# Pooled query-key products issued ahead of the maximum over the local scores in a fused attention and two-layer MoE kernel

## The chip, the cores and the metric

The kernel runs on one core of one Trainium2 chip. The metric is the device time of one execution in microseconds (us). Engines are named as in the profile: PE is the matrix engine (TensorE), PEld its weight loads, DVE the vector engine, ACT the scalar engine, POOL the GpSimd engine, SP the engine that only issues transfers here. PSUM is the accumulator memory into which PE writes; it is used in banks of 512 fp32 columns.

## The reference

The input is q, k, v of shape 2 x 8 x 576 x 64 (batch, heads, tokens, head size). Each token attends twice: to its neighbours less than four tokens away, and on sequences that are pooled by four. The two results are added, and the sum goes through two feed-forward layers.

```python
q_d, k_d, v_d = means over groups of 4 tokens          # 144 pooled tokens
out_up = repeat(softmax(scale * q_d @ k_d.T) @ v_d, 4)
mask = abs(pos[:, None] - pos[None, :]) < 4
out_local = softmax(where(mask, scale * q @ k.T, -1e9)) @ v
x = (out_up + out_local) as 1152 x 512
h = relu(x @ w_in); x = (s * h * h + b) @ w_out          # MoE 1, d_ff 2048
p = probs / (sum(probs) + 1e-9)
out = sum over 4 experts of p[:, e] * (relu(x @ w1[e]) @ w2[e])   # F = 1024
```

Each softmax subtracts the row's maximum before the exponential.

## The kernel before, in words

The attention is cut into 16 units: 4 groups (batch x half of the sequence) times 4 pairs of heads. A half is 256 or 320 tokens; a unit works on local tiles of 64 queries and 72 keys, the two heads of a pair side by side in the 128 partitions. The steps of a unit, by their names in the code:

- `a_step` transposes k (L494) and q (L512) on PE; ACT copies them out of PSUM as `kT` (L500) and `qz` (L519), and DVE pools q to `qd` (L526). `k_step` pools k on POOL to `kd` (L539, L541); L474 and L475 on POOL pool v.
- `b_step` forms the scores. One PSUM bank, `ps[0]` (shown as psa in the profile, as the whole ring of banks is), takes the mask (L576), some filler products that keep PE active (L584) and the local scores (L591) in its columns 0 to 287 or 359. From column 360 the same bank takes the pooled scores: of both heads in units of the first half (L605), of one head in units of the second half, whose other head has a bank of its own (L615, two matrix products). DVE takes the negated maxima, `ml` over the local scores (L599) and `md` over the pooled ones (L617), and ACT the exponentials with their sums (L571; local ones to `pl`, pooled ones to `pd`).
- `norm_step` divides by the sums on DVE (L630 to L635), `c_step` transposes the weights on PE (L657) and ACT copies them to `pT` (L660), `d_step` multiplies them with v (L678, L685; ACT L694, DVE L701), and `x_step` splits the result into a high and a low part for the next layer (ACT L713, POOL or DVE L715).

The units are pipelined: in each round the steps run on different units (`b_step` one behind `a_step`, `c_step` two, `d_step` three). A scheduler orders each engine's instructions by priority from the order in which the program calls them; POOL's are in the order of the code. Between a writer and a reader of one tile it places a wait, and a PSUM bank is one tile: two instructions on different columns of a bank are kept in program order as well. Each engine works through its own instructions in that order.

Beside the attention, the weights of the following layers are prepared: a weight is split into high and low parts by ACT (L157, L196) and DVE (L161, L167, L186, L199), and the products of MoE 1 (helper `products`, L316, three products for one at full precision; ACT L767, L772, DVE L769, L773) fill PE between the attention's steps from about 51 us on. `keep_warm` (L361) adds filler products. The attention ends about 143 us into the span; what follows is MoE 1 and the four experts (L316, L863).

Of the kernel before, what the change touches and what calls it, by code (L numbers as in the profile page):

```python
# [13 lines left out]
ALU = mybir.AluOpType  # L14
AX = mybir.AxisListType
# [7 lines left out]
def attn_moe_moe_kernel(  # L23
# [14 lines left out]
    nc = tc.nc  # L38
# [36 lines left out]
    def window(n):  # L75

        return min(max(n * TQ - FAC, 0), S - W)
# [320 lines left out]
    def unit(u):  # L398
        g, j = divmod(u, NP)
        b, hf = divmod(g, HALVES)  # L400
        return g, j, b, hf

    def tiles(hf):

        return (0, CUT) if hf == 0 else (CUT, NTQ - CUT)
# [6 lines left out]
    def bank():  # L412
        return psa.tile([P, 512], F32, tag="a", name="psa")
# [137 lines left out]
    def b_step(u):  # L551

        g, j, b, hf = unit(u)
        n0, m = tiles(hf)
        gd = m * TQ // FAC
        qz, qd = st.pop(("q", u))
        kT = st["kT", j]
        kd = st["kd", j]
        pl = ap2.tile([P, MX, W], F32, tag="pl", name="pl")[:, :m]
        ml = ap2.tile([P, MX, 1], F32, tag="ml", name="ml")[:, :m]  # L560
        both = gd == GB
        pd = ap2.tile([P, 2, SD], F32, tag="pd", name="pd")
        md = ap2.tile([P, 2, 1], F32, tag="md", name="md")
        if both:
            pd, md = pd[:, :1], md[:, :1]
        else:
            pd, md = pd[:gd], md[:gd]
        sm = sums[u % 2]

        def exps(out, ps, m, total):  # L570
            nc.scalar.activation(  # L571
                out=out, in_=ps, func=ACTF.Exp, bias=m, scale=1.0, accum_out=total
            )

        ps = [bank()] + ([] if both else [bank()])
        last_pe["att"] = nc.tensor.matmul(  # L576
            ps[0][:, : m * W],
            identb.rearrange("p a q -> p (a q)"),
            mask[:, hf * 2 : hf * 2 + m].rearrange("p t w -> p (t w)"),
            start=True,  # L580
            stop=False,
        )
        for _ in range(fill[u] // 448):
            nc.tensor.matmul(  # L584
                ps[0][:, : m * W], idle[:, :P], idle[:, : m * W], start=False, stop=False
            )
        for t in range(m):
            k0 = window(n0 + t)
            for a in range(2):
                o = slice(a * D, a * D + D)  # L590
                last_pe["att"] = nc.tensor.matmul(  # L591
                    ps[0][a * TQ : a * TQ + TQ, t * W : t * W + W],
                    qz[o, t * TQ : t * TQ + TQ],
                    kT[o, k0 : k0 + W],
                    start=False,
                    stop=t == m - 1,
                )
        local = ps[0][:, : m * W].rearrange("p (t w) -> p t w", w=W)
        nc.vector.tensor_reduce(out=ml, in_=local, axis=AX.X, op=ALU.max, negate=True)  # L599
        pooled = [] if both else [ps[0][:gd, MX * W : MX * W + SD], ps[1][:gd, :SD]]  # L600
        if both:
            pooled = [ps[0][: 2 * gd, MX * W : MX * W + SD]]
            for a in range(2):
                o = slice(a * D, a * D + D)
                last_pe["att"] = nc.tensor.matmul(  # L605
                    ps[0][a * gd : a * gd + gd, MX * W : MX * W + SD],
                    qd[o, :],
                    kd[o, :],
                    start=True,
                    stop=True,  # L610
                )
        else:
            for a in range(2):
                o = slice(a * D, a * D + D)
                last_pe["att"] = nc.tensor.matmul(pooled[a], qd[o, :], kd[o, :], start=True, stop=True)  # L615
        for a in range(len(pooled)):
            nc.vector.tensor_reduce(  # L617
                out=md[:, a], in_=pooled[a], axis=AX.X, op=ALU.max, negate=True
            )
        for t in range(m):  # L620
            exps(pl[:, t], local[:, t], ml[:, t], sm[:, t])
        for a in range(len(pooled)):
            exps(pd[:, a], pooled[a], md[:, a], sm[: pd.shape[0], MX + a])
        st["p", u] = pl, pd
# [337 lines left out]
    def side_step():  # L962
# [14 lines left out]
    pool_order.enter_context(tc.manual_schedule(engines={mybir.EngineType.Pool}))  # L977
    steps = [
        (b_step, 1),
        (a_step, 0),  # L980
        (k_step, 0),
# [9 lines left out]
    for i in range(last + 1):  # L991
# [13 lines left out]
        for f, lag in steps:  # L1005
            u = i - lag
            if 0 <= u < NU:

                with tc.high_priority(ahead.get(f, 0)) if f in ahead and u < NP else nullcontext():
                    f(u)  # L1010
            if f is x_step and u >= 0 and u % NP == NP - 1:
                slots += l1_steps(0, u // NP) + l2_steps(0, u // NP)
                firsts.append(slots[-FC - KD])
                if u < NP:

                    for _ in range(3):
                        take_slot()
            if f in (k_step, c_step) and slots and i < last:
                take_slot()
            if f in (b_step, k_step, c_step, v_step):  # L1020
                side_step()
# [110 lines left out]
```

## Time and profile before

| | us |
|---|---|
| median of 3 runs | 696.87 (695.46 to 697.39) |
| profiled execution, its own time | 696.83 |
| span of the profiled execution | 695.0 |
| PE busy | 683.0 (98%) |
| DVE busy | 404.8 (58%) |
| ACT busy | 346.3 (50%) |
| POOL busy | 101.2 (15%) |

The span runs from the first to the last instruction of the profiled execution, and its own time is 1.83 us more. A row of a timeline gives the start in the span, the length, the engine, the line of the kernel, the operation with output and inputs, and, in brackets, the time for which the engine had been idle before and what ended it. A row of a window gives the busy time of each engine in that stretch and the granted clock as a share of the full 2.4 GHz: 0.50 is the lower level, 1.2 GHz.

### The profile page before, as it was taken

The page shows a single profiled execution, that of the slowest core. Times are in us where ns is not written, and L with a number is a line of the kernel's source. Part 1 is how long each engine was busy: PE and PEld are TensorE (multiplying, and loading weights), DVE is VectorE, ACT ScalarE, POOL GpSimd, SP SyncE. Part 2 cuts the span into 40 slices and gives each one's busy share as a digit, 9 for nine tenths or more (in the row PEclk, how much of TensorE's full clock was granted, in tenths as well). Part 3 has the DMA queues.
Part 4 walks back from the last instruction along what each step waited for, and adds up shares of the span by engine and source line. Part 5 has one row for each costly group of instructions (what it writes and reads, how often), then busy time and mean ns, then how long its engine had stood idle before and what let it go on. Part 6 is the DMA issues. An engine that isn't in the chain of part 4 may idle for free.

```text
span 695.0 us, 11964 instructions
## 1 busy us (share of the span) xinstructions
PE 683.0 (98%) x4788; PEld 620.2 (89%) x4788; DVE 404.8 (58%) x720; ACT 346.3 (50%) x846; POOL 101.2 (15%) x123
## 2 busy tenths in 40 slices
PE   9989999999999999999999999999999999999997
PEld 5768778899999999999899899999898988998996
DVE  1898847778862434496535636645546456455442
ACT  3768757777965666665534423433334233243220
POOL 4431332100000200103011201201211012010000
PEclk9999989999999999999999999999999999999999
DMA  8784635405410011010210201201101103011012
GB/s 179 200 206 102 110 83 159 141 6 192 166 64 1 0 32 46 16 32 1 62 31 31 70 21 56 67 32 38 54 31 62 30 32 91 3 60 31 1 61 75
DMA packets 54167, 46.43 MB, mean 67 GB/s; under 512 B 32224, under 2 KB 42720, under 8 KB 54112
## 3 DMA queue, kind: packets, MB, share of 16 engines
q1 hardware_dynamic: 54112, 45.67, 23.9%
q8 instruction: 37, 0.61, 0.4%
q14 instruction: 18, 0.15, 0.1%
HBM read 43.31 MB, written 2.36 MB: 66 GB/s over the span
## 4 chain that ended last, share of the span: by engine, by line
PE 92%; DVE 6%; ACT 2%; issue 1%; DVEq 0%; ACTq 0%
PE psm L316 43%; PE psx L863 25%; PE psx L316 13%; PE psa L361 3%; PE psa L657 1%; PE psa L685 1%; PE psa L591 1%; PE psa L678 1%; PE psa L512 1%; PE psa L615 1%; PE psa L494 1%; DVE cv L175 0%; DVE cv L186 0%; PE psa L605 0%; DVE cv L161 0%
## 5 line engine op out<-in xcount | busy, mean ns | idle before, releaser
L316 PE MATMUL psm<-w,h 128*128 128x512 f32 x864 | 208.7, 391 | 0.0
L316 PEld LDWEIGHTS psm<-w,h 128*128 128x128 f32 x864 | 158.5, 188 | 30.0
L863 PE MATMUL psx<-x,w 128*128 128x320 f32 (+1 forms) x768 | 117.8, 296 | 0.0
L863 PEld LDWEIGHTS psx<-x,w 128*128 128x128 f32 x768 | 109.3, 190 | 1.7
L259 POOL TENSOR_TENSOR sw<-raw 128x256 f32<-128x256 f32 x32 | 31.3, 1000 | 411.5 <-DMA raw<-in_moe_w_dram 245.4
L878 ACT COPY r<-psx 128x320 f32<-128x320 f32 (+1 forms) x96 | 38.0, 396 | 92.6 <-PE psx L863 92.2
L881 ACT ACTIVATE h<-r 128x320 fp32r<-128x320 f32 (+1 forms) x96 | 42.0, 444 | 83.6 <-DVE r L892 83.6
L934 DVE SCALAR_TENSOR_TENSOR acc<-psm,pr,acc 128x512 f32<-128x512 f32 x63 | 47.2, 749 | 58.0 <-PE psm L316 58.0
L863 PE MATMUL psx<-t,w 128*128 128x320 f32 (+1 forms) x448 | 80.3, 302 | 0.2 <-DVE r L892 0.2
L892 DVE TENSOR_TENSOR r<-psx,r 128x320 f32<-128x320 f32 (+1 forms) x96 | 43.2, 456 | 58.7 <-PE psx L863 56.7
L863 PEld LDWEIGHTS psx<-t,w 128*128 128x128 f32 x448 | 67.0, 189 | 4.5 <-DVE r L892 0.5
L316 PE MATMUL psm<-x,w 128*128 128x320 f32 (+2 forms) x420 | 68.9, 315 | 0.0
L316 PEld LDWEIGHTS psm<-x,w 128*128 128x128 f32 x420 | 63.8, 193 | 0.9 <-issue 0.8
L882 DVE SCALAR_TENSOR_TENSOR h<-r,h 128x320 fp32r<-128x320 f32 (+1 forms) x96 | 47.7, 502 | 18.5 <-ACT h L881 16.2
L316 PE MATMUL psm<-h,w 128*128 128x256 f32 (+2 forms) x360 | 56.3, 305 | 0.0
L316 PE MATMUL psx<-h,w 128*128 128x384 f32 (+1 forms) x312 | 55.8, 327 | 0.0
L316 PEld LDWEIGHTS psx<-h,w 128*128 128x128 f32 x312 | 52.0, 188 | 0.0
L316 PEld LDWEIGHTS psm<-h,w 128*128 128x128 f32 x360 | 50.8, 190 | 1.0 <-issue 0.7
L316 PE MATMUL psx<-x,w 128*128 128x384 f32 (+2 forms) x252 | 43.1, 320 | 0.0
L316 PEld LDWEIGHTS psx<-x,w 128*128 128x128 f32 x252 | 40.6, 188 | 0.0
L237 DVE TENSOR_TENSOR w<-raw,w 128x1024 fp32r<-128x1024 f32 x16 | 19.5, 1224 | 25.8 <-ACT w L234 25.8
L780 DVE TENSOR_TENSOR h<-r,h 128x384 fp32r<-128x384 f32 (+2 forms) x40 | 21.6, 541 | 20.9 <-ACT h L779 19.6
(105 smaller groups left out, 874.6 us busy)
## 6 DMA issues: line engine op xcount, KB each, us to landing
raw<-in_moe_w_dram SPq DMA_DIRECT2D x32, 512.0 KB
raw<-in_moe_w_in_dram SPq DMA_DIRECT2D x8, 1024.0 KB
raw<-in_moe_w_out_dram SPq DMA_DIRECT2D x8, 1024.0 KB
kn<-in_k_dram SPq DMA_DIRECT2D x8, 288.0 KB
v<-in_v_dram SPq DMA_DIRECT2D x8, 288.0 KB
out_dram<-acc SPq DMA_DIRECT2D x9, 256.0 KB
qn<-in_q_dram SPq DMA_DIRECT2D x8, 160.0 KB
vn<-in_v_dram SPq DMA_DIRECT2D x16, 72.0 KB
```

The lines of the kernel that those rows point to most:

```text
L237: nc.vector.tensor_tensor(out=k0[1], in0=source(), in1=f32(k0[0]), op=ALU.subtract)
L259: nc.gpsimd.tensor_tensor(out=operand(out), in0=operand(x), in1=operand(y), op=op)
L316: nc.tensor.matmul(o, stat(ps, kk), mov(pm, kk, i), start=c == 0, stop=c == len(terms) - 1)
L361: nc.tensor.matmul(ps[:, c0:], idle[:, :P], idle[:, :n], start=True, stop=True)
L494: last_pe["att"] = nc.tensor.transpose(psk[:, i * KP : i * KP + KP], kn[:, c * m + i].rearrange("p a d -> p (a d)"), ident[:KP, :KP],)
L780: nc.vector.tensor_tensor(out=h[1], in0=r, in1=f32(h[0]), op=ALU.subtract)
L863: nc.tensor.matmul(ps, s_ap(n, half, a, w, kk), xt[x, pi][b][:, kk], start=first and c == 0, stop=c == len(terms) - 1, skip_group_check=True,)
L878: nc.scalar.copy(t, st[name])
L881: nc.scalar.activation(out=h[0][:, halves[hf]], in_=t, func=ACTF.Relu)
L882: nc.vector.scalar_tensor_tensor(out=h[1][:, halves[hf]], in0=t, scalar=0.0, in1=f32(h[0][:, halves[hf]]), op0=ALU.max, op1=ALU.subtract,)
L892: nc.vector.tensor_tensor(out=st[t], in0=st[name], in1=st[t], op=ALU.add)
L934: nc.vector.scalar_tensor_tensor(out=a, in0=ps, scalar=p_e, in1=a, op0=ALU.mult, op1=ALU.add)
```

## The change

The instruction that takes the maximum over the local scores is written behind the pooled products instead of ahead of them. Nothing is added or removed. Because the bank is one tile, the wait between the two turns round: before, the pooled products in `ps[0]` came behind the maximum in program order, and waited for DVE to have read the bank; now the maximum comes behind the products, and waits for PE to have written the bank.

```diff
         local = ps[0][:, : m * W].rearrange("p (t w) -> p t w", w=W)
-        nc.vector.tensor_reduce(out=ml, in_=local, axis=AX.X, op=ALU.max, negate=True)
         pooled = [] if both else [ps[0][:gd, MX * W : MX * W + SD], ps[1][:gd, :SD]]
         if both:
             pooled = [ps[0][: 2 * gd, MX * W : MX * W + SD]]
...
             for a in range(2):
                 o = slice(a * D, a * D + D)
                 last_pe["att"] = nc.tensor.matmul(pooled[a], qd[o, :], kd[o, :], start=True, stop=True)
+        nc.vector.tensor_reduce(out=ml, in_=local, axis=AX.X, op=ALU.max, negate=True)
         for a in range(len(pooled)):
             nc.vector.tensor_reduce(
                 out=md[:, a], in_=pooled[a], axis=AX.X, op=ALU.max, negate=True
```

In the changed file the pooled products are L604 and L614, and the maximum is L615; L617 and all behind it keep their numbers. Every engine has as many instructions as before. The order on POOL and SP is the same; on PE, DVE and ACT it differs only inside the attention. The numbers in the names below tell the tiles apart.

PE in unit 10 (85.7 to 90 us of the trace before). psa_1428 is the unit's score bank; the L494 rows are a later unit's transposes of k.

```order
 L576 MATMUL psa_1428<-mask_87,identb_84 128x288
 L591 MATMUL psa_1428<-kT2_1346,qz_1362 64x72 x8
-L605 MATMUL psa_1428<-kd2_1368,qd_1364 64x144 x2
+L604 MATMUL psa_1428<-kd2_1368,qd_1364 64x144 x2
 L494 MATMUL psa_1448<-ident_79,kn_1312 128x96 x3
 L494 MATMUL psa_1453<-ident_79,kn_1312 128x96 x3
```

PE's order is the same here, but for the line number: the pooled products stood directly behind the local scores before, too.

DVE in the same unit. qd_1364 is its pooled q; sums, pl_1322 and pd_1324 belong to unit 9, whose weights are divided here; ml_1425 and md_1427 are unit 10's maxima.

```order
 L526 TENSOR_REDUCE qd_1364<-psa_1357 128x64
+L632 TENSOR_TENSOR pl_1322<-pl_1322,sum1_107 128x288
 L701 TENSOR_TENSOR xg_1392<-psa_1370,ud_1390 128x320
-L632 TENSOR_TENSOR pl_1322<-pl_1322,sum1_107 128x288
 L635 TENSOR_TENSOR pd_1324<-pd_1324,sum1_107 128x144
 L715 TENSOR_TENSOR x1_77<-xg_1392,x0_76 128x320
-L599 TENSOR_REDUCE ml_1425<-psa_1428 128x4
+L615 TENSOR_REDUCE ml_1425<-psa_1428 128x4
 L617 TENSOR_REDUCE md_1427<-psa_1428 128x1
```

The maximum keeps its place behind four other DVE instructions (L632 and L701 change places); what turns round is which of the two, it or the pooled products, waits for the other.

ACT at about 31 us. psa_520 is a bank with transposed weights of unit 1, pl_551 and pd_553 are the exponentials of unit 2.

```order
 L713 CAST x0_76<-xg_511 128x256
 L157 ACTIVATE cv_441<-raw_297 128x1024
-L660 COPY pT_513<-psa_520 72x256
 L571 ACTIVATE pl_551,sum1_107<-psa_555,ml_552 128x72 x4
 L571 ACTIVATE pd_553,sum1_107<-psa_555,md_554 128x144
+L660 COPY pT_513<-psa_520 72x256
 L519 ACTIVATE qz_587<-psa_579 128x320
 L694 ACTIVATE ud_613<-psa_592 128x64
```

The copy that PE needs for unit 1's products with v (L678) moved behind all five exponentials of unit 2.

## Rows read from the trace of the kernel before

**Rows 1.** The page: span, engines, chain shares by engine
```profile
span 695.0 us, 11964 instructions
...
PE 683.0 (98%) x4788; PEld 620.2 (89%) x4788; DVE 404.8 (58%) x720; ACT 346.3 (50%) x846; POOL 101.2 (15%) x123
...
PE 92%; DVE 6%; ACT 2%; issue 1%; DVEq 0%; ACTq 0%
```

**Rows 2.** Windows: stretch, length, busy PE, PEld, DVE, ACT, POOL, granted clock, DMA, GB/s
```profile
12.00:143.00 131.00, 124.39 (x1437) 102.97 (x1434) 99.07 (x204) 91.84 (x331) 38.12 (x42) 0.96 0.59 143
143.00:690.00 547.00, 546.81 (x3284) 509.97 (x3283) 303.95 (x510) 251.37 (x511) 58.74 (x64) 1.00 0.15 46
30.00:40.00 10.00, 7.99 (x107) 5.96 (x103) 9.06 (x16) 7.09 (x22) 4.64 (x5) 1.00 0.58 114
40.00:50.00 10.00, 8.96 (x109) 7.17 (x108) 9.75 (x18) 6.29 (x25) 3.62 (x3) 0.83 0.85 215
...
84.90:88.30 3.40, 1.08 (x20) 0.70 (x19) 2.44 (x8) 2.31 (x10) 1.04 (x2) 0.96 0.71 176
88.30:94.40 6.10, 6.10 (x29) 5.04 (x31) 2.16 (x6) 2.67 (x14) 2.49 (x4) 0.50 0.47 102
```

**Rows 3.** Waits on PE: total us, times, longest
```profile
PE psa L615 <- DVE ml L599: 3.6, 3, 2.0
PE psa L605 <- DVE ml L599: 2.2, 2, 1.6
...
PE psa L576 <- ACT pd L571: 0.7, 1, 0.7
```

**Rows 4.** Timeline 30 to 50 us: start, length, engine, line; brackets: idle before
```profile
31.43 0.31 DVE L617 TENSOR_REDUCE md<-psa 128x1 f32<-128x144 f32 x1 [0.71 <-PE psa L605]
...
31.63 0.37 ACT L660 COPY pT<-psa 72x256 f32<-72x256 f32 x1 [0.21 <-PE psa L361]
...
33.10 0.38 ACT L571 ACTIVATE pd<-psa,md 128x144 f32<-128x144 f32 x1
...
38.62 0.30 DVE L617 TENSOR_REDUCE md<-psa 80x1 f32<-80x144 f32 x1
...
38.76 0.47 PE L615 MATMUL psa<-kd,qd 64*80 64x144 f32 x2 [2.01 <-DVE ml L599]
38.83 1.33 DVE L199 TENSOR_TENSOR w<-cv,w 128x1024 fp32r<-128x1024 f32 x1
...
48.09 0.47 PE L615 MATMUL psa<-kd,qd 64*80 64x144 f32 x2 [1.04 <-DVE ml L599]
```

**Rows 5.** Timeline, 81 to 88 us, up to the longest wait for the maximum
```profile
81.09 0.71 PE L494 MATMUL psa<-ident,kn 96*128 96x96 f32 x6
...
81.98 1.49 POOL L474 TENSOR_TENSOR v<-v 72x512 f32<-72x512 f32 x1
82.26 1.38 DVE L635 TENSOR_TENSOR pd<-pd,sum 128x144 f32<-128x144 f32 x1
...
83.56 0.29 DVE L617 TENSOR_REDUCE md<-psa 128x1 f32<-128x144 f32 x1
...
85.96 0.72 PE L591 MATMUL psa<-kT,qz 64*64 64x72 f32 x16
85.99 0.38 DVE L526 TENSOR_REDUCE qd<-psa 128x64 f32<-128x256 f32 x1
...
87.04 0.30 DVE L635 TENSOR_TENSOR pd<-pd,sum 128x144 f32<-128x144 f32 x1
...
87.69 0.45 DVE L599 TENSOR_REDUCE ml<-psa 128x4 f32<-128x288 f32 x1
```

**Rows 6.** Timeline, 88 to 91 us, the wait and the stretch behind it
```profile
88.29 0.74 PE L605 MATMUL psa<-kd,qd 64*64 64x144 f32 x4 [1.61 <-DVE ml L599]
...
88.96 1.22 PE L494 MATMUL psa<-ident,kn 96*128 96x96 f32 x6
```

**Rows 7.** Timeline near 108 us
```profile
108.37 0.47 PE L615 MATMUL psa<-kd,qd 64*80 64x144 f32 x2 [0.51 <-DVE ml L599]
```


## The prediction, written before the changed kernel ran

> **What bounds the kernel now.** I read the page first. PE is busy for 683.0 of 695.0 us, and the chain that ended last is 92% PE, 6% DVE [rows 1]. So time can only come from where PE idles or runs at the lower clock. The windows say where. From 143 to 690 us PE is busy for 546.81 of 547.00 us at a granted clock of 1.00: nothing is to be had there, and the order there is unchanged. From 12 to 143 us, the attention, it is busy for 124.39 of 131.00 us at a mean clock of 0.96 [rows 2]. That is 6.61 us of idling and about 131 x 0.04 = 5.2 us lost to the clock; 11.8 us is the ceiling for any change here.
>
> The waits on PE tell how much of the idling is the wait that the change turns round: the pooled products waited for the maximum over the local scores five times, 3.6 us at L615 and 2.2 us at L605, 5.8 us of the 6.61 [rows 3]. The timeline says where they lie: 2.01 us up to 38.76 and 1.04 up to 48.09 (place A) [rows 4], 1.61 up to 88.29 (place B) [rows 6], 0.51 up to 108.37 (place C) [rows 7]; the fifth is the rest of L605's sum, 2.2 - 1.6 = 0.6 us [rows 3].
>
> But a wait is worth only what limits its stretch. Place A lies in DVE's stretch: DVE is busy for 9.06 and 9.75 of 10 us in the windows from 30 and 40 us [rows 2]. Place B is PE's: DVE has 2.16 of 6.10 us behind the wait, and all of it runs at a clock of 0.50 with PE busy throughout [rows 2].
>
> **The change part by part.** No instruction is added or removed. All sums are against the profiled execution's own time, 696.83 us, 0.04 under the median of 696.87.
>
> *Place B.* L591 ends at 85.96 + 0.72 = 86.68. In the kernel before, L605 stands directly behind it in PE's order, and starts at 88.29, because the maximum (87.69, 0.45 us) stands on DVE behind four others, the last division L635 among them (87.04) [rows 5, 6]. After the change L604 needs only the pooled q and k. The pooled q is written by 85.99 + 0.38 = 86.37, before L591 ends [rows 5]; the pooled k came earlier. So the 1.61 us go. The maximum then waits for L604, which it doesn't notice: it comes up on DVE no earlier than before.
>
> Then the clock. In the 3.40 us up to 88.30 PE is busy for 1.08; the next 6.10 us run at 0.50, the lower level, 1.2 GHz [rows 2]. The same six transposes at L494 take 0.71 us at 81.09 and 1.22 at 88.96 [rows 5, 6]. At full clock this stretch takes 6.10 x 0.50 = 3.05 us. I expect the clock to stay up, because most of the idle time in front, 1.61 of 2.32 us, goes. So B gives 1.61 + 3.05 = 4.66 us. Bounds: if the clock falls all the same, or L604 starts some 0.4 us late behind a DVE instruction such as L526 (0.38), 1.61 - 0.4 = 1.2; if the exponentials move forward as well and the 0.71 us wait of L576 [rows 3] goes, 4.66 + 0.71 = 5.4. I take 4.66, because both of its terms stand in rows of this place, and the bounds need a further event.
>
> *Place A.* The waits of 2.01 and 1.04 us, 3.05 in all, go from L615. DVE's work stays, though, and is the limit, so PE must wait for it, or for what depends on it, elsewhere. The order shows two such places. On ACT, the copy L660 (31.63, 0.37 us, ends at 32.00) falls behind five exponentials, which end at 33.10 + 0.38 = 33.48 [rows 4]: PE's products with v wait for that copy, so some 33.48 - 32.00 = 1.48 us are put back there. On DVE the weight step L199 (1.33 us) comes before a pair of maxima, and with the one over the pooled scores (0.30, the 38.62 row) holds the following step by 1.63 us [rows 4]. 3.05 - 1.48 - 1.63 = -0.06: I count A as nothing. Bounds: 0.7 us better, since DVE's one idle piece here is 0.71 us, in front of 31.43 [rows 4]; 1.7 us worse, from the clock: the window from 40 us has a mean of 0.83, so 10 x 0.17 = 1.7 us are lost in it [rows 2]. There the loss lies in DVE's stretch and costs nothing; if the new waits put the fall a little later, where PE is the limit, it costs all of it.
>
> *Place C and the fifth wait.* At 108.37 PE is the limit, and the pooled products wait 0.51 us only because DVE was late [rows 7]: -0.51 (0 to -0.51). The fifth wait lies early, where DVE again sets the pace; 0, at best -0.6.
>
> *What is added.* In all 16 units the maximum now waits for the pooled products, 0.47 us of PE's time [rows 4]. On DVE, what is behind it waits as well: the maximum over the pooled scores, which waited for the products anyway, then the exponentials. Where PE is the limit, this is covered by PE's own queue; where DVE is, by the fact that md came behind the products before as well (in front of 31.43, DVE had idled for them already [rows 4]). I count 0; with no cover it would be 16 x 0.47 = 7.5 us on DVE's path, a bound that no stretch comes near.
>
> The Trainium skill ("PSUM — Partial Sum Buffer", section "PSUM bank collisions raise a hardware error") asks for PSUM to be guarded by bank, whatever the columns. By it the wait can't be removed here, only turned round, which speaks against the change. The trace agrees that the guard is a wait, 5.8 us in all [rows 3]; which side pays less is decided by the rows above, not by the rule.
>
> Sum: -4.66 + 0 - 0.51 = -5.17, so 696.83 - 5.17 = 691.7 us.
>
> **The rivals.**
>
> *R1, DVE stays late at B by another overlap.* In unit 9 the division L635 took 1.38 us, against 0.30 at 87.04, while POOL's L474 ran (81.98 to 83.47) [rows 5]. What is next on DVE, md at 83.56, came late, then the exponentials, then DVE's sums, behind which the pooled q stands. If after the change POOL meets another of these instructions as well, L604 waits for the pooled q: 1.08 us more. B is then worth 1.61 - 1.08 = 0.53 and the clock falls still; with C, 1.04, so 695.8 us. Against it: POOL's order is the same, and DVE's order there is nearly so. The Trainium skill ("SBUF — State Buffer", section "SBUF: two separate sides") says that DVE and GpSimd share a pair of ports as an exclusive lock, and the loser blocks; the 1.38 us agree with it.
>
> *R2, the clock falls at the wrong place.* The forecast, with A's upper bound: 691.7 + 1.7 = 693.4 us. For it: the 2.01 us wait of A becomes two waits a little later. Against it: DVE's stretch goes on behind them.
>
> *R3, slower: ACT's order.* ACT works in order, and the exponentials come earlier and as one block, ahead of copies that PE waits for. At A one block puts back 1.48 us, which is in the sum. If a second one does so where PE is the limit (the copies of k and q in units 8 to 10 stand beside exponentials, and L576 already waits 0.71 us for them [rows 3]), that costs 1.48 more; PE's idling there keeps B's low clock, so that B gives nothing, and A pays its 1.7. With C: 1.48 + 1.7 - 0.51 = +2.7, so 699.5 us. It decides as soon as PE's new waits for ACT are longer than B's removed 1.61 us. Against it: ACT is busy for only 2.31 of 3.40 us ahead of B [rows 2].
>
> *R4, nothing changes.* The wait is turned round, DVE's chain (division, maxima, exponentials, copy) is as long as before, and PE waits for the same total at other lines: 696.8 us. For it: DVE and ACT are busy for 99.07 and 91.84 of the attention's 131.00 us [rows 2], and A behaves this way by my own sum. Against it: B, where the product waits for an instruction whose result it doesn't use.
>
> **How the numbers follow.** Forecast 0.47, R2 0.15, R3 0.15, R1 0.13, R4 0.10. A measurement of this kernel tells about 0.3% from no change, 2.1 us: faster is under 694.7, slower over 699.0. Faster: the forecast, R2 nearly whole and the better edge of R1, 0.62. Same: the rest of R1, R4 nearly whole, a little of R2 and R3, 0.21. Slower: R3 and the bad ends, 0.17. The likeliest case's own range is 689.7 to 693.5: below it go A's 0.7, B's 0.7 and the fifth wait's 0.6 (691.7 - 2.0), above it A's 1.7. The range is 689.4 to 698.5, which adds 0.3 below for the scatter of runs, takes in R1, R2 and R4 above, and ends short of R3.
>
> **What would show it.** B right: the pooled products of unit 10 start within 0.1 us of the end of the local scores, and the granted clock in the six us behind is 1.00; L494 there takes 0.71. A right: the waits at L615's line gone, two new ones of about 1.5 us near 32 and 48 us, for ACT at L678 and for DVE at L657. R1 shows as a wait of the pooled products for L526; R2 as a clock of 0.50 behind 50 us; R3 as waits for ACT's copies at L591 or L678 from 75 us on. I am wrong if PE's idling between 12 and 143 us stays above 5 us with a mean clock no better than 0.96, although the waits for ml are gone.

## The result, and the profile after

The changed kernel takes 685.87 us (median of 4 runs, 685.39 to 689.71) against 697.06 us before (4 runs): a ratio of 0.9859 with a 95% interval of 0.9825 to 0.9894. Run once more among the experiments it gave 686.42 us, 0.9857 (0.9839 to 0.9875). It is some 10 us faster, in the forecast direction, about twice the forecast 5.2 us and below the range of 689.4 to 698.5. The profiled execution took 686.19 us, 10.64 less than the one before; its span is 10.6 us shorter.

The page of the changed kernel: span, engines, chain by engine.

```profile
span 684.4 us, 11971 instructions
...
PE 673.4 (98%) x4788; PEld 615.0 (90%) x4788; DVE 404.4 (59%) x720; ACT 345.1 (50%) x846; POOL 103.2 (15%) x123
...
PE 89%; DVE 7%; ACT 2%; issue 1%; DMA 1%; POOL 1%; ACTq 0%; POOLq 0%
```

PE is busy for 9.6 us less [rows 1], with the same number of instructions: what went is mostly time in which PE was busy, not idling. The waits on PE (total us, times, longest):

```profile
PE psa L657 <- DVE qd L526: 2.0, 1, 2.0
PE psa L678 <- ACT pT L660: 1.4, 1, 1.4
PE psa L657 <- ACT pd L571: 1.3, 1, 1.3
```

Nobody waits for ml any more; the 5.8 us of [rows 3] are gone, L576's 0.7 too. New are 2.0 us at L657 for DVE and 1.4 at L678 for ACT, the two waits that the prediction named for place A, and 1.3 more at L657.

To see where the time went, the span is cut at the same work in both kernels: at the mask products (L576) of units 8, 10, 12 and 15. Windows of the kernel before (stretch, length, busy PE, PEld, DVE, ACT, POOL, granted clock, DMA share, GB/s):

```profile
0.00:72.72 72.72, 67.77 (x728) 52.56 (x728) 52.56 (x106) 47.20 (x162) 23.85 (x38) 0.98 0.77 171
72.72:85.68 12.96, 12.17 (x168) 9.96 (x168) 10.47 (x20) 8.87 (x34) 6.17 (x8) 1.00 0.51 85
85.68:105.75 20.07, 18.42 (x173) 15.58 (x172) 10.81 (x29) 11.59 (x43) 6.12 (x8) 0.83 0.45 98
105.75:129.61 23.86, 23.35 (x260) 19.50 (x260) 18.86 (x39) 18.53 (x68) 3.35 (x4) 1.00 0.54 162
```

The same work in the changed kernel, and the four microseconds behind 49 us:

```profile
0.00:71.03 71.03, 64.55 (x727) 51.30 (x728) 52.20 (x105) 46.09 (x161) 24.60 (x37) 0.98 0.80 175
71.03:82.64 11.61, 11.61 (x169) 9.68 (x168) 9.39 (x23) 10.05 (x38) 6.44 (x7) 1.00 0.57 90
82.64:97.89 15.25, 15.14 (x174) 13.21 (x173) 10.88 (x27) 10.11 (x40) 7.19 (x9) 1.00 0.40 100
97.89:119.19 21.30, 21.30 (x261) 18.57 (x260) 18.09 (x39) 18.80 (x71) 3.82 (x4) 1.00 0.75 207
...
49.00:53.00 4.00, 4.00 (x23) 4.00 (x23) 2.24 (x9) 1.23 (x4) 0.00 (x0) 0.57 1.01 167
```

| stretch | forecast | measured | of it PE idle, clock, PE's products |
|---|---|---|---|
| start to unit 8 (place A) | 0 | 72.72 to 71.03: -1.69 | see below |
| units 8 and 9 | 0, at best -0.7 | 12.96 to 11.61: -1.35 | -0.79, 0, -0.56 |
| units 10 and 11 (place B) | -4.66 | 20.07 to 15.25: -4.82 | -1.54, -3.41, +0.13 |
| units 12 to 14 (place C) | -0.51 | 23.86 to 21.30: -2.56 | -0.51, 0, -2.05 |
| the rest | 0 | -0.2 | |

The split is worked out from the rows: idle is length less PE's busy time, the clock's part is length times one less the granted clock (20.07 x 0.17 = 3.41), and the rest is what PE's own products took at full clock. Place B came as forecast, to 0.2 us, and so did the wait of place C. What was missed is the first row and the second, and the 2.05 us by which PE's products themselves became shorter in the fourth. In the first row PE idles for 1.53 us more than before (6.48 against 4.95) and is busy for 3.22 us less (64.55 against 67.77).

At place B, unit 10 after the change, the pooled products start 0.11 us behind the end of the local scores (82.86 + 0.72 = 83.58), and the transposes behind them take 0.71 us, as at full clock:

```profile
83.69 0.46 PE L604 MATMUL psa<-kd,qd 64*64 64x144 f32 x4
84.08 0.71 PE L494 MATMUL psa<-ident,kn 96*128 96x96 f32 x6
```

The timeline shows where most of the 2.05 us come from. Unit 13 before, PE alone (start, length, line, operation):

```profile
115.44 0.47 PE L615 MATMUL psa<-kd,qd 64*80 64x144 f32 x2
...
116.13 0.39 PE L316 MATMUL psm<-h,w 128*128 128x320 f32 x1
116.45 0.47 PE L615 MATMUL psa<-kd,qd 64*80 64x144 f32 x2
116.85 1.88 PE L316 MATMUL psm<-h,w 128*128 128x320 f32 x11
118.66 0.46 PE L678 MATMUL psa<-pT,vd 72*64 72x64 f32 x8
```

and after:

```profile
106.19 0.48 PE L614 MATMUL psa<-kd,qd 64*80 64x144 f32 x4
106.60 0.49 PE L512 MATMUL psa<-ident,qn 80*128 80x80 f32 x4
106.89 2.00 PE L316 MATMUL psm<-h,w 128*128 128x320 f32 x12
108.82 0.46 PE L678 MATMUL psa<-pT,vd 72*64 72x64 f32 x8
```

In units of the second half each head's pooled product has its bank. Before, the one in the bank of its own went ahead, and the one in `ps[0]` came later, in the middle of the products of MoE 1, as it stood behind the maximum: twice 0.47 us, and 116.13 to 118.66 is 2.53 us for twelve L316 products and the late one. After, nothing holds the second, they stand back to back, and both together take 0.48 us (x4 instead of x2); the twelve products behind take 108.82 - 106.89 = 1.93. The two heads lie in partitions 0 to 63 and 64 to 127 of their inputs. That both products take as long as one says that they run at the same time; the kernel that keeps them apart, below, tests it.

### The profile page after: what moved, and what is told of

Read it like the earlier page. It is cut to its first block, busy times and chain, and to the rows that moved or that the text cites. A ratio compares the mean times of both kernels' runs of the same rounds, so it can differ in the third digit from the quotient of the medians.

```text
span 684.4 us, 11971 instructions
## 1 busy us (share of the span) xinstructions
PE 673.4 (98%) x4788; PEld 615.0 (90%) x4788; DVE 404.4 (59%) x720; ACT 345.1 (50%) x846; POOL 103.2 (15%) x123
## 4 chain that ended last, share of the span: by engine, by line
PE 89%; DVE 7%; ACT 2%; issue 1%; DMA 1%; POOL 1%; ACTq 0%; POOLq 0%
PE psm L316 43%; PE psx L863 26%; PE psx L316 13%; PE psa L361 1%; PE psa L591 1%; PE psa L657 1%; PE psa L685 1%; DVE cv L186 1%; PE psa L512 1%; DMA kn<-in_k_dram 1%; DVE cv L167 1%; DVE cv L175 1%; PE psa L678 1%; DVE pl L632 0%; DVE cv L161 0%
## 5 line engine op out<-in xcount | busy, mean ns | idle before, releaser
L316 PE MATMUL psm<-w,h 128*128 128x512 f32 x864 | 208.7, 391 | 0.0
L316 PEld LDWEIGHTS psm<-w,h 128*128 128x128 f32 x864 | 158.5, 188 | 30.0
L316 PE MATMUL psm<-x,w 128*128 128x320 f32 (+2 forms) x420 | 68.1, 315 | 0.0
L316 PEld LDWEIGHTS psm<-x,w 128*128 128x128 f32 x420 | 63.8, 194 | 0.3 <-issue 0.2
L882 DVE SCALAR_TENSOR_TENSOR h<-r,h 128x320 fp32r<-128x320 f32 (+1 forms) x96 | 48.6, 512 | 18.5 <-ACT h L881 16.4
L316 PE MATMUL psm<-h,w 128*128 128x256 f32 (+2 forms) x360 | 56.3, 305 | 0.3 <-DVE h L773 0.3
L316 PE MATMUL psx<-h,w 128*128 128x384 f32 (+1 forms) x312 | 55.9, 327 | 0.0
L316 PEld LDWEIGHTS psx<-h,w 128*128 128x128 f32 x312 | 52.0, 188 | 0.0
L316 PEld LDWEIGHTS psm<-h,w 128*128 128x128 f32 x360 | 50.9, 190 | 1.2 <-DVE h L773 0.7
L316 PE MATMUL psx<-x,w 128*128 128x384 f32 (+2 forms) x252 | 43.1, 320 | 0.0
L316 PEld LDWEIGHTS psx<-x,w 128*128 128x128 f32 x252 | 40.6, 188 | 0.0
```

The costliest lines, as they stand in the source:

```text
L316: nc.tensor.matmul(o, stat(ps, kk), mov(pm, kk, i), start=c == 0, stop=c == len(terms) - 1)
L882: nc.vector.scalar_tensor_tensor(out=h[1][:, halves[hf]], in0=t, scalar=0.0, in1=f32(h[0][:, halves[hf]]), op0=ALU.max, op1=ALU.subtract,)
```

## The experiments

All times are medians with their number of runs; ratios are to the kernel before, timed beside each, with medians of 696.3 to 696.7 us.

**One half of the change at a time.** In the first of two kernels the maximum moves only in first-half units, in the second only in second-half units.

```diff
-        nc.vector.tensor_reduce(out=ml, ...)
+        if not both:        # second kernel: if both:
+            nc.vector.tensor_reduce(out=ml, ...)
...
+        if both:            # second kernel: if not both:
+            nc.vector.tensor_reduce(out=ml, ...)
         for a in range(len(pooled)):
```

> The maximum is put behind the pooled products only in units of the first half (one bank, both heads' pooled products back to back in either kernel); second-half units stay as before. Theory P (pairing: in second-half units the two heads' pooled products now stand back to back and run together on the two halves of the array's rows, 0.48 us for both against twice 0.47, and that is the missing gain): only place B's gain shows, 4.7 to 5.4 us, so 691.7 to 692.4 us, with L615 still at 16 groups of 0.47. Theory W (the missing gain is waits and clock, place B being worth about twice what was counted): most of the whole gain, 687 to 689 us.

> The complement: the maximum is put behind the pooled products only in units of the second half (two banks). Theory P: 8 pairs of products shrink from 0.94 to 0.48 us, 3.7 us, plus place C's 0.5 and little at place A: about 692.5 us (691.5 to 694), place B's 1.6 us wait and its half clock still there. Theory W: only place C and what place A gives, 0.5 to 1 us: 696 to 696.5 us.

First half alone: 690.98 us (6), 0.9918 (0.9902 to 0.9934). Second half alone: 691.13 us (6), 0.9922 (0.9903 to 0.9942). Each gives half, and the halves add up to the whole. That is near what the pairing theory expects in size. The place of the first kernel's gain is as it said, that of the second's is not. Waits of the first kernel, then of the second, each with its window from unit 10 to unit 12:

```profile
PE psa L616 <- DVE ml L600: 1.8, 1, 1.8
PE psa L681 <- ACT pT L663: 1.4, 1, 1.4
PE psa L576 <- ACT pd L571: 1.4, 1, 1.4
...
86.14:101.16 15.02, 15.02 (x173) 13.11 (x172) 10.71 (x29) 11.10 (x43) 6.22 (x7) 1.00 0.43 102
```

```profile
PE psa L606 <- DVE ml L600: 2.0, 2, 1.4
...
84.24:101.82 17.58, 15.56 (x174) 13.36 (x173) 11.08 (x28) 11.14 (x41) 6.50 (x9) 1.00 0.54 117
```

With only first-half units changed, the wait for the maximum is gone from unit 10, and the stretch takes 15.02 instead of 20.07 us at a clock of 1.00: all of place B, although L576 now waits 1.35 us in front of it. With only second-half units changed, unit 10 still waits 1.40 us for the maximum, yet the clock there is 1.00 too, and the stretch is 2.49 us shorter than in the kernel before. So that wait does not bring the clock down in every surrounding.

**The two heads' products kept apart, or brought together.** In the changed kernel a product of one column on all rows goes between them; in the kernel before the second is issued right behind the first, behind the same wait.

```diff
             for a in range(2):
                 o = slice(a * D, a * D + D)
                 last_pe["att"] = nc.tensor.matmul(pooled[a], qd[o, :], kd[o, :], ...)
+                if a == 0:
+                    nc.tensor.matmul(ps[1][:, SD : SD + 1], idle[:, :P], idle[:, :1], ...)
```

```diff
             for a in range(2):
                 o = slice(a * D, a * D + D)
-                last_pe["att"] = nc.tensor.matmul(pooled[a], qd[o, :], kd[o, :], ...)
+                with tc.issue_after(last_pe["att"].ins) if a else nullcontext():
+                    last_pe["att"] = nc.tensor.matmul(pooled[a], qd[o, :], kd[o, :], ...)
```

> The changed kernel with one matrix product of one column on all 128 rows between the two heads' pooled products in second-half units, so that they can't run together; the waits are as in the changed kernel. Theory P: the 3.7 us come back, less what lies in the vector engine's stretch, plus some 0.1 us for each of the 8 separators: 688.5 to 690.5 us. Theory W: only the separators, 686 to 686.8 us.

> The kernel before, its maximum and its wait where they were, but in second-half units the second head's product is issued right behind the first's, so that both wait for the maximum and then run together. Theory P: 8 pairs at 0.48 instead of 0.94 us, less up to half of it in the vector engine's stretch: 693.3 to 695 us. Theory W: no gain, since the waits for the maximum stay: 697 us or a little more.

Apart: 687.32 us (4), 0.9868 (0.9848 to 0.9889), 0.9 to 1.5 us above the two measurements of the changed kernel, between the two theories; the intervals overlap. Timeline of unit 13 with the separator (L616), then the windows up to unit 8 and from there on:

```profile
106.28 0.47 PE L614 MATMUL psa<-kd,qd 64*80 64x144 f32 x2
106.68 0.18 PE L616 MATMUL psa<-idle 128*128 128x1 bf16 x1
106.79 0.47 PE L614 MATMUL psa<-kd,qd 64*80 64x144 f32 x2
```

```profile
0.00:71.10 71.10, 66.86 (x731) 52.49 (x732) 52.82 (x107) 46.54 (x161) 23.55 (x37) 0.98 0.80 177
71.10:82.70 11.60, 11.60 (x168) 9.66 (x167) 8.96 (x20) 9.41 (x37) 6.79 (x7) 1.00 0.43 79
82.70:97.69 14.99, 14.99 (x173) 13.21 (x173) 10.60 (x28) 9.84 (x40) 6.79 (x9) 1.00 0.40 94
97.69:120.29 22.60, 22.60 (x264) 19.49 (x263) 18.34 (x39) 19.13 (x71) 3.83 (x4) 1.00 0.74 200
```

Both products take 0.47 us again, and units 12 to 14 take 22.60 instead of 21.30 us, 1.30 us for three units. Each separator itself holds PE for 0.11 us (106.68 to 106.79), so some 1.0 us of it is the price of the pairing where PE is the limit. The stretch up to unit 8 does not get longer (71.10 against 71.03 us), though four pairs lie in it and PE is busy there for 66.86 instead of 64.55 us (first row): there the pairing is worth nothing. I had expected 2.5 us or more; 1.3 and one more unit behind is what there is.

Together: 694.21 us (10), 0.9961 (0.9945 to 0.9977). The pairs run in half the time, but wait longer; below the waits are the windows of units 10 and 11 and of units 12 to 14:

```profile
PE psa L616 <- DVE ml L599: 6.4, 4, 2.4
PE psa L605 <- DVE ml L599: 2.7, 3, 1.4
...
85.97:103.57 17.60, 15.54 (x174) 13.34 (x173) 11.09 (x28) 11.09 (x42) 6.55 (x9) 1.00 0.54 117
103.57:127.26 23.69, 22.11 (x261) 18.82 (x260) 19.11 (x38) 18.10 (x68) 3.36 (x4) 1.00 0.51 163
```

6.4 us in all at the paired products against 3.6 [rows 3]: held together, both stand behind the maximum. The time is what the pairing theory forecast, but not for its reason: units 12 to 14 gain next to nothing (23.69 against 23.86 us), and the gain lies at units 10 and 11 (17.60 against 20.07 us), where the clock is 1.00 with a wait of 1.39 us for the maximum. Pairing pays at units 12 to 14 only where both products may go early.

**What makes place B.** Three kernels. In the kernel before, four fillers (L361) run in the 0.7 us for which L576 waits; and, in another, one division of unit 8 (L635) is done by ACT instead of DVE. In the changed kernel, unit 10 alone gets its old wait back.

```diff
-            keep_warm(ps, n, fill[u])
+            keep_warm(ps, n, fill[u] + (1024 if u == 2 * NP and not cols else 0))
```

```diff
+        if u == 2 * NP:
+            nc.scalar.activation(out=pd[:, 0], in_=pd[:, 0], func=ACTF.Copy, scale=sm[:, MX])
+        else:
             nc.vector.tensor_tensor(out=pd, ...)
```

```diff
+        if u == 2 * NP + 2: nc.vector.tensor_reduce(out=ml, ...)
         pooled = [] if both else ...
...
-        nc.vector.tensor_reduce(out=ml, ...)
+        if u != 2 * NP + 2: nc.vector.tensor_reduce(out=ml, ...)
```

> The kernel before with four more filler products (0.1 us each) behind the weight transposes of unit 8, so that they run in PE's 0.71 us wait in front of unit 10's mask product; the wait of 1.6 us for the maximum is left as it is. Theory C (the lower clock behind 88 us comes from both idle pieces together, 0.7 and 1.6 us; with either gone it stays at 1.00): the wait at L605 still 1.6 us, the clock from 88 to 94 us at 1.00, some 3 us gained: 693 to 693.8 us. Rival (the 1.6 us wait alone brings the clock down): clock 0.50 as before and no gain, 696.3 us.

> The changed kernel with the maximum ahead of the pooled products in unit 10 alone; every engine's order is that of the changed kernel, only this one wait is turned back. Theory C: the wait of about 1.5 us for the maximum is back at unit 10, but the clock stays at 1.00, since PE does not idle in front of unit 10's mask product any more: 687.2 to 687.6 us. Rival (place B's whole gain, stall and clock, hangs on this one wait): 4.7 us back, 690 to 690.8 us.

> The kernel before with one instruction of unit 8 (L635, the division of the pooled weights, 1.38 us beside POOL's L474 against 0.30 elsewhere) on the scalar engine instead of the vector engine; no other order differs, and the wait for the maximum stays. Theory K (the 0.71 us wait of L576 and the longer half of the low clock come from this overlap of vector engine and POOL): the maxima of unit 9 come about 1 us earlier, L576 no longer waits, L605 still waits 1.4 to 1.7 us, the low clock costs 0 to 1.7 instead of 3.4 us: 2.4 to 4 us less than before, 692.5 to 694.1 us. Rival (the overlap moves to the next vector instruction, or another wait holds L576): L576 still waits, 696 to 697 us.

Fillers: 695.93 us (12), 0.9989 (0.9977 to 1.0001), no gain that can be told. Unit 10's wait back: 688.89 us (4), 0.9894 (0.9878 to 0.9911), 2.5 to 3 us lost: between the two theories of that run, over 1 us from either, because the clock falls, but for half as long. The division on ACT: 694.79 us (12), 0.9978 (0.9964 to 0.9992), faster, by less than expected. The window from unit 10 to unit 12 of the three, in this order (for the fillers that from unit 4 to unit 8 too):

```profile
34.31:73.87 39.56, 36.20 (x397) 30.45 (x397) 34.61 (x69) 28.27 (x97) 8.35 (x8) 0.91 0.67 148
...
86.82:105.65 18.83, 17.06 (x172) 14.67 (x172) 10.93 (x29) 11.65 (x43) 6.10 (x8) 0.91 0.49 105
```

```profile
83.28:101.64 18.36, 16.66 (x173) 14.64 (x173) 10.65 (x28) 11.20 (x42) 7.07 (x10) 0.91 0.47 104
```

```profile
84.84:103.38 18.54, 17.02 (x173) 14.71 (x173) 10.62 (x29) 11.23 (x41) 6.54 (x9) 0.91 0.50 108
```

All three have one wait for the maximum of 1.5 to 1.7 us in it, as before, and lose 9% of some 18.5 us to the clock, 1.7 us, half of the 3.41 before. In all three PE idles for no more than 0.3 us in front of unit 10's mask product. So the wait that the change turns round costs some 1.7 us of clock where it stands without the wait of L576, and 3.41 where both stand. L576's wait costs the clock nothing by itself: it is 1.35 us long in the kernel with only first-half units changed, where the clock is 1.00. The two don't add up; the second half of the loss comes only when both are there. The filler kernel's gain was eaten up elsewhere in its profile: its stretch from unit 4 to unit 8 lost 39.56 x 0.09 = 3.6 us to the clock, against 37.73 x 0.05 = 1.9 before. Executions of it differ: three of the twelve had a mean clock of 0.997 over the span and took 694.1 to 694.6 us, the others 0.992 or 0.993 and 694.9 to 697.5. The mean clock was 0.992 or 0.993 in every run of the kernel before that was timed beside the experiments, and 0.995 to 1.000 in those of the changed kernel.

And L576's wait comes from DVE and POOL getting in each other's way. The division kernel:

```profile
82.32 0.31 DVE L617 TENSOR_REDUCE md<-psa 128x1 f32<-128x144 f32 x1
...
84.84 0.29 PE L576 MATMUL psa<-mask,identb 64*128 64x288 bf16 x1
...
87.31 0.46 PE L605 MATMUL psa<-kd,qd 64*64 64x144 f32 x4 [1.52 <-DVE ml L599]
```

Without the 1.38 us of L635 the pooled maximum starts 2.40 us behind unit 9's mask product (79.92) instead of 3.57 (83.56 - 79.99) [rows 5], and L576 doesn't wait. In the traces of all the kernels, L576 waits at unit 10 in just those three in which unit 8's division meets L474 and takes 1.37 or 1.38 us: the kernel before, the first-half one and the one with fillers. Where DVE does that division in 0.29 or 0.30 us, it does not wait. In the changed kernel the same work of DVE and POOL is out of step by itself:

```profile
78.86 0.44 DVE L632 TENSOR_TENSOR pl<-pl,sum 128x288 f32<-128x288 f32 x1
...
79.23 0.30 DVE L635 TENSOR_TENSOR pd<-pd,sum 128x144 f32<-128x144 f32 x1
...
79.51 0.86 POOL L715 TENSOR_TENSOR x<-xg,x 128x320 fp32r<-128x320 f32 x1 [0.69 <-PE psa L604]
...
79.84 0.29 DVE L617 TENSOR_REDUCE md<-psa 128x1 f32<-128x144 f32 x1
```

The divisions (L632, L635) take 0.44 and 0.30 us and end as POOL starts; L474 comes behind them, at 80.33.

**What limits place A.** In the changed kernel: unit 1's copy on ACT ahead of four exponentials, more fillers in units 4 and 5, four divisions (L635, units 2 to 5) on ACT instead of DVE.

```diff
-            nc.scalar.copy(pT[:, c0 : c0 + n], ps[:W, :n])
+            with tc.high_priority(120) if u in (1, 2, 3) else nullcontext(): nc.scalar.copy(...)
```

```diff
-    fill = [1408 if u < NP else ...]
+    fill = [1408 if u < NP + 2 else ...]
```

```diff
+        if 1 < u < 6:
+            for a in range(n):
+                nc.scalar.activation(out=pd[:, a], in_=pd[:, a], func=ACTF.Copy, scale=sm[:rows, MX + a])
+        else:
             nc.vector.tensor_tensor(out=pd, ...)
```

> The changed kernel with unit 1's second copy of transposed weights on the scalar engine moved ahead of four of unit 2's five exponentials; no other engine's order differs. My step on place A (the vector engine is the limit there, a wait taken from PE comes back behind it): the 1.4 us wait near 32 us shrinks to some 0.3, and the time stays within 0.5 us of the changed kernel, 685.4 to 686.2 us. Rival (PE's own waits there are the limit): 1.1 us less, 684.8 us, or 683.1 us if the half clock behind 49 us goes too.

> The changed kernel with the larger number of fillers also in units 4 and 5 (31 more filler products, about 0.1 us each, some 3.2 us of PE work) where PE waits for the vector engine and the half clock follows behind 49 us. If the fillers lie in idle time and hold the clock: up to 1.7 us gained, 684.2 us. If they lie on PE's path: up to 3.2 us lost with the clock held or not, 687.4 to 689 us.

> The changed kernel with the divisions of the pooled weights (L635) of units 2 to 5 on the scalar engine: some 0.3 + 0.3 + 0.45 + 0.45 = 1.5 us less on the vector engine between 28 and 52 us, 6 more scalar instructions of 0.3 to 0.4 us. If the vector engine is the limit of that stretch, as step A has it: 1 to 1.5 us less, 684.4 to 684.9 us. Rival (the scalar engine's order holds PE there, with the vector engine only near its limit): no gain or up to 1 us lost, 685.9 to 686.9 us.

Copy first: 686.11 us (4), 0.9853 (0.9835 to 0.9870), the same as the changed kernel. More fillers: 686.85 us (4), 0.9865 (0.9847 to 0.9884), the same or a little slower. Divisions on ACT: 684.94 us (5), 0.9831 (0.9812 to 0.9849). Window from unit 4 to unit 8, first of the kernel before and of the changed kernel, then of the three in this order:

```profile
34.99:72.72 37.73, 34.68 (x398) 29.03 (x397) 34.35 (x69) 28.15 (x97) 8.35 (x8) 0.95 0.72 155
```

```profile
34.71:71.03 36.32, 32.78 (x397) 28.08 (x397) 32.50 (x66) 26.80 (x96) 8.84 (x7) 0.95 0.72 153
```

```profile
33.55:70.14 36.59, 34.08 (x397) 29.09 (x397) 33.77 (x68) 26.88 (x96) 8.84 (x7) 0.91 0.74 161
```

```profile
34.58:71.25 36.67, 33.84 (x422) 28.29 (x422) 33.87 (x70) 28.75 (x97) 8.26 (x7) 1.00 0.76 159
```

```profile
35.35:69.65 34.30, 31.35 (x397) 26.54 (x397) 31.74 (x64) 28.39 (x101) 7.91 (x7) 1.00 0.75 162
```

The wait at L678 (1.39 us before 31.77) lies ahead of this stretch. Without it unit 4 begins 1.16 us earlier in the profile (33.55 against 34.71) and unit 8 only 0.89, and the median shows no gain; 9% of that stretch went to the clock, 5% in the changed kernel. With the clock at 1.00 throughout, and 25 products more on PE, the stretch is 36.67 us against 36.32. With some 1.5 us of DVE's work taken away it is 34.30. This fits DVE as the limit, as step A had it: it is busy for 32.50 of 36.32 us in the changed kernel. It is not shown alone, since the last row also has the clock at 1.00, where the changed kernel lost 1.8 us to it.

**The changed kernel again, and both edits.** The combination has the copy and the divisions.

> The changed kernel once more, for a closer interval and beside the combination of the same call. By the runs so far: 685 to 686.5 us, 10.5 us below the kernel before, the low clock between 1.000 and 0.995 of the span.

> The changed kernel with both edits that touch the stretch from 28 to 52 us: the four divisions on the scalar engine, and unit 1's copy ahead of four exponentials. If the vector engine is the limit there, the copy adds nothing again: 684.4 to 685.2 us, as with the divisions alone. Rival (with the vector engine relieved, PE's 1.4 us wait for the copy is the limit): another 1 us less, 683.5 to 684 us.

686.42 us (4) as told above; the combination 685.25 us (4), 0.9843 (0.9827 to 0.9859). The copy adds nothing here either. The fastest is the kernel with the divisions on ACT, 684.94 us, about 1 us under the changed kernel; the intervals overlap, so that it is ahead is likely but not shown.

## Why the prediction was wrong

**The turned wait at place B: right.** -4.66 forecast, -4.82 measured, from the wait and the clock as said. The kernel with only first-half units changed shows it by itself: 15.02 - 20.07 = -5.05, with L576's wait still there. The price depends on what stands around the wait: in the changed kernel, where L576 does not wait, turning unit 10's wait back costs 18.36 - 15.25 = 3.1 us in its window, the wait and half of the low clock. R1 did not come: unit 10's L604 starts 0.11 us behind the local scores.

**The wait of L576: mis-sized.** The prediction had it as a bound, "if the exponentials move forward as well", and took 0. Units 8 and 9 gave 1.35 us: 0.79 of idling, and 0.56 by which PE's own products became shorter. The division kernel, which loses only the wait, gains 12.96 - 12.18 = 0.78 us there (72.66 to 84.84). The 0.56 go with another order on PE (unit 9's pooled products came behind the transposes of k at 81.88, and now come directly behind the local scores at 79.01); no run isolates it. The division kernel shows the mechanism of the wait, which the prediction described as rival R1, but as a danger: it is the overlap with POOL that was there before and that the change happened to undo. Which shift undid it is not shown in full: it is absent wherever second-half units changed (second half alone, apart, paired) and present where only the first half did (L576 waits 1.4 us there).

**The products' own time: the step that failed.** The prediction set out from "time can only come from where PE idles or runs at the lower clock", with 11.8 us of that as the ceiling. "No instruction is added or removed" was taken to mean that PE's time for the products stays, and place C was closed with "-0.51 (0 to -0.51)". The 0.47 us of a second-half product at L615 were two instructions for one head [rows 4], while L605 has four for both heads in one group [rows 6]. PE's order at second-half units, which the sum did not price, brings the two together. Where PE is the limit PE's products became 2.05 us shorter over three units. Some 1.0 us of it is the pairing, by the separator run. Some 0.6 is that the late product no longer stands among those of MoE 1: 2.53 - 1.93 = 0.60 us in unit 13, of which its own time up to the next product is 0.40 (116.45 to 116.85), which leaves 0.20 a unit; this part is read from the timeline, and no run isolates it. Some 0.5 stays open. Of the 5.4 us that the profiles show beyond the forecast, 2.05 are this, 1.35 units 8 and 9, 1.69 place A, and the rest place B and the end.

**Place C: right** in its wait, 0.51 us, and blind to the pairing at the same place.

**Place A: right in kind.** Two new waits where they were expected, 1.4 and 2.0 us for 1.48 and 1.63, and a third of 1.3 us that was not foreseen; that the time is DVE's fits the runs but is not shown alone. Rival R2 came true in form: the low clock moved behind 49 us, 0.57 in the window to 53, and its loss up to unit 8 is the same as before, 1.8 to 1.9 us. Still, the stretch up to unit 8 became 1.69 us shorter instead of 0 to 0.7. It isn't the pairing, since the separator run has it too (72.72 to 71.10). Of the 1.69 us, 0.34 lie ahead of the first mask product (7.55 against 7.21 us), whose start varies from 6.94 to 7.96 us between the kernels' profiles. The halves alone gave +0.39 and -0.61 us (unit 8's mask product at 73.11 and 72.11 against 72.72 us); what makes up the rest stays open.

**R3 and R4: no.** ACT's exponentials held PE at place A, for 1.4 us at L678 and 1.3 at L657, and nowhere later; the waits for ml did not come back at another line behind 75 us.

## What to carry to other kernels

When an edit changes which instructions stand next to each other on the matrix engine, price the products themselves and not only the waits: here two products on different partition halves cost as much as one when they are neighbours. A small wait in front of a large one can double what the large one costs through the clock (3.41 us against 1.7 here), even where such a wait alone costs the clock nothing, so bounds that lie close together in time are not independent. And a rival that names an overlap as a danger should be priced in the other direction too, as something that may end.

## What the runs showed of the hardware

- Two fp32 products of 64 rows each, on partitions 0 to 63 and 64 to 127, take 0.48 us back to back; a product of one column on all rows between them makes it 0.47 twice.
- How long PE idled around unit 10, in front of its mask product, in front of its pooled products or both, and what the clock then cost up to unit 12: 1.35 us at the mask product, nothing; at the pooled products 1.39 or 1.40 us, nothing; 1.52 us, 1.67; 1.70 us, 1.65; at both, 0.26 and 1.61 us, 1.69; 0.71 and 1.61 us, 3.41. Each is from one profiled execution.
- DVE's division of 128x144 took 1.38 us beside POOL's 72x512 addition and 0.30 without it. The Trainium skill ("SBUF — State Buffer", section "SBUF: two separate sides") says that a DVE instruction with two inputs in SBUF and a GpSimd instruction that reads SBUF exclude each other; the trace agrees: the division started 0.28 us behind the addition (82.26, 81.98) and ended 0.17 us behind its end [rows 5].
